# Block products with seven multiplications in layer 1 of a routed MLP, with layer 2 computed for two experts at a time

## The chip, the cores and the metric

One core of a Trainium2 chip. The metric is the device time of one execution in microseconds, the median over runs. A profile is one such execution with every instruction recorded; its span is about 2 us shorter than the time. The granted clock is the share of TensorE's full clock that the profile records; "half clock" below means that it was 0.5.

Names used below: PE is TensorE (matmuls), PEld its weight loads, DVE is VectorE, ACT is ScalarE, POOL is GpSimd, SP is SyncE, which issues DMAs.

## The reference

Sliding-window attention (8 batches of 576 tokens, 8 heads of 64) gives x, 4608 tokens by 512. Then a dense mixture of 8 experts, weighted by a matrix P that eight rounds of row and column normalisation (Sinkhorn) produce:

```python
P = np.exp(logits - logits.max())
for _ in range(8):
    P /= P.sum(1, keepdims=True) + 1e-09
    P /= P.sum(0, keepdims=True) + 1e-09
    P *= N / E
for e in range(8):
    h = np.maximum(x @ w1[e], 0.0)      # layer 1: 512 -> 1024
    out += P[:, e:e + 1] * (h @ w2[e])  # layer 2: 1024 -> 512
```

## The kernel before

Expert 0 is computed during and just after the attention, without P. Then experts 1 to 7 run over 9 groups of 512 tokens: 63 steps. In a step, layer 1 of the *next* step is woven between the products of layer 2 of this one. P is positive, so x is multiplied by it before layer 1. Layer 2 already uses the Winograd form of Strassen's method: hidden activations and w2 are cut into 2 x 2 blocks, and seven block products instead of eight give the result, with sums S (S1 to S4) of activations and T of weights made on DVE. `rebase` takes one quarter of a group's running result off another quarter, so that the products can be added to it; `settle` adds it back at the end.

```python
def make_xs(i):                      # x * P, P in fp32
    for d2 in range(2):
        nc.vector.tensor_tensor(out=xss[i][:, 2*d2:2*d2+2, :], in0=xT[:, 2*d2:2*d2+2, ...],
                                in1=Pb.unsqueeze(1).to_broadcast([P, 2, GT]), op=ALU.mult)

def l1s(i, ft):                      # layer 1, plain: 8 x 4 matmuls of 512 columns a step
    for dt in range(NDT):
        nc.tensor.matmul(out=psh, lhsT=w1ts[e][:, dt, P*ft:P*ft+P], rhs=xss[i][:, dt, :], ...)
    nc.scalar.activation(out=hTs[i][:, ft, :], in_=psh, func=AF.Relu)

def product(i, m):                   # layer 2: one of seven products, 8 matmuls of 256 columns
    ...

def gather(i, bank, rh, ch, op):     # add a product's bank to the running result
    if (rh, ch) != (1, 1) and e < E - 1:
        nc.scalar.copy(out=st, in_=banks[bank])                # ACT: PSUM -> SBUF
        nc.gpsimd.dma_start(out=t, in_=st, accum_op=ALU.add)   # DMA adds
        return
    nc.vector.tensor_tensor(out=t, in0=t, in1=banks[bank], op=op)
# [cut] the loop: product 1, piece of layer 1, product 7, piece, 5, piece, 6, piece, 2, ...
```

The whole kernel:

The softmax here doesn't subtract the row's maximum and nothing guards it: scores larger than these inputs give would overflow.

## Time and profile before

| | |
|---|---|
| time | 1088.22 us (6 runs, 1084.86 to 1091.17) |
| span of the profile | 1083.1 us |
| attention, up to the last gate matmul | 207.8 us |
| first layer-1 matmul of expert 1 | 250.8 us |
| one step | 13.02 us |
| last layer-1 matmul; last matmul | 1066.2; 1073.8 us |

The page's first lines give busy time, share of the span and instructions per engine:

```profile
span 1083.1 us, 18767 instructions
## 1 busy us (share of the span) xinstructions
PE 1047.4 (97%) x7675; PEld 670.9 (62%) x7675; DVE 694.1 (64%) x1072; ACT 542.7 (50%) x959; POOL 270.2 (25%) x264
```

The chain of waits, followed back from the last instruction, as the page sums it up by engine:

```profile
PE 93%; DVE 2%; DMA 1%; ACT 1%; issue 1%; DVEq 0%; POOL 0%; ACTq 0%; SPq 0%; POOLq 0%
```

And two pieces of the same chain in order of time (start, duration, engine, what and line), the runs of eight layer-1 matmuls where one step meets the next:

```profile
569.27 1.73 PE psh L577 x8
582.29 1.73 PE psh L577 x8
```

So TensorE bounds the kernel, and a step is 582.29 - 569.27 = 13.02 us.

Groups of instructions (line, engine, operation, output and inputs, shapes, count; busy us and mean ns of one; idle time just before them and what ended it):

```profile
L577 PE MATMUL psh<-xs,w1t 128*128 128x512 f16 x2016 | 506.3, 379 | 0.5 <-DVE xs L564 0.5
...
L649 ACT COPY st<-M 128x512 f32<-128x512 f32 x162 | 94.0, 580 | 0.0
...
L564 DVE TENSOR_TENSOR xs<-xT,Pb 128x1024 f16<-128x1024 f16 x126 | 148.2, 1218 | 1.0 <-DMA Pb<-PTd 1.0
...
L601 DVE TENSOR_TENSOR S<-hT 128x1024 f16<-128x1024 f16 x126 | 86.7, 688 | 198.9 <-ACT hT L584 198.9
...
L652 DVE TENSOR_TENSOR acc_lo<-acc_lo,M 128x512 f32<-128x512 f32 x186 | 127.1, 683 | 61.6 <-PE M L635 61.6
```

The stretches view of the steady loop (stretch, length, then busy us and instructions of PE, PEld, DVE, ACT, POOL; granted clock, DMA share, GB/s):

```profile
400.00:500.00 100.00, 100.00 (x677) 65.95 (x675) 59.45 (x82) 46.52 (x85) 29.02 (x25) 1.00 0.53 87
```

PE never stops there; DVE and ACT have 40% and 53% of their time free. That free time is what the change spends.

### The profile page before, as it was taken

The page shows a single profiled execution, that of the slowest core. Times are in us where ns is not written, and L with a number is a line of the kernel's source. Part 1 is how long each engine was busy: PE and PEld are TensorE (multiplying, and loading weights), DVE is VectorE, ACT ScalarE, POOL GpSimd, SP SyncE. Part 2 cuts the span into 40 slices and gives each one's busy share as a digit, 9 for nine tenths or more (in the row PEclk, how much of TensorE's full clock was granted, in tenths as well). Part 3 has the DMA queues.
Part 4 walks back from the last instruction along what each step waited for, and adds up shares of the span by engine and source line. Part 5 has one row for each costly group of instructions (what it writes and reads, how often), then busy time and mean ns, then how long its engine had stood idle before and what let it go on. Part 6 is the DMA issues. An engine that isn't in the chain of part 4 may idle for free.

```text
span 1083.1 us, 18767 instructions
## 1 busy us (share of the span) xinstructions
PE 1047.4 (97%) x7675; PEld 670.9 (62%) x7675; DVE 694.1 (64%) x1072; ACT 542.7 (50%) x959; POOL 270.2 (25%) x264
## 2 busy tenths in 40 slices
PE   4899999899999999999999999999999999999996
PEld 2655555445666666666666666666666666666664
DVE  5877776656666755565556555565556555667885
ACT  3666666456666544444444444444444444443331
POOL 6332230010332322223222323232222323220000
PEclk9999999999999999999999999999999999999998
DMA  9978761424455594449444765559444944443323
GB/s 172 158 77 77 72 67 8 81 32 111 80 85 84 90 159 79 79 78 155 80 82 84 124 121 85 83 85 156 79 78 79 156 79 85 83 61 105 104 93 97
DMA packets 123334, 101.36 MB, mean 94 GB/s; under 512 B 46288, under 2 KB 107120, under 8 KB 123248
## 3 DMA queue, kind: packets, MB, share of 16 engines
q0 software_dynamic: 107968, 73.44, 50.8%
q1 hardware_dynamic: 14848, 26.34, 7.8%
q8 instruction: 60, 0.98, 0.4%
q10 hardware_dynamic: 432, 0.39, 0.1%
q14 instruction: 26, 0.21, 0.1%
HBM read 79.02 MB, written 9.58 MB: 82 GB/s over the span
## 4 chain that ended last, share of the span: by engine, by line
PE 93%; DVE 2%; DMA 1%; ACT 1%; issue 1%; DVEq 0%; POOL 0%; ACTq 0%; SPq 0%; POOLq 0%
PE psh L577 40%; PE M L635 35%; PE psh L110 6%; PE psy L124 5%; PE psS L219 3%; PE psN L267 2%; ACT pt L227 1%; PE psT_q L187 1%; PE psT_k L187 1%; PE psXT L307 1%; DMA qf<-in_q_dram 1%; DVE xsb L276 1%; DMA PTd<-PT_sb 0%; DVE acc_hi L652 0%; DVE QZ L206 0%
## 5 line engine op out<-in xcount | busy, mean ns | idle before, releaser
L584 ACT ACTIVATE hT<-psh 128x512 f16<-128x512 f32 x504 | 301.9, 599 | 424.9 <-PE psh L577 423.3
L577 PE MATMUL psh<-xs,w1t 128*128 128x512 f16 x2016 | 506.3, 379 | 0.5 <-DVE xs L564 0.5
L577 PEld LDWEIGHTS <-w1t 128*128 128x128 f16 x2016 | 197.2, 98 | 145.9 <-issue 0.8
L635 PEld LDWEIGHTS <-S 128*128 128x128 f16 x2016 | 197.2, 98 | 75.8
L601 DVE TENSOR_TENSOR S<-hT 128x1024 f16<-128x1024 f16 x126 | 86.7, 688 | 198.9 <-ACT hT L584 198.9
L650 POOL DMA_DIRECT2D acc_lo<-st x108 | 128.8, 1211 | 339.7 <-ACT st L649 339.2
L635 PEld LDWEIGHTS <-hT 128*128 128x128 f16 x1512 | 147.9, 98 | 59.3 <-issue 3.1
L652 DVE TENSOR_TENSOR acc_lo<-acc_lo,M 128x512 f32<-128x512 f32 x186 | 127.1, 683 | 61.6 <-PE M L635 61.6
L564 DVE TENSOR_TENSOR xs<-xT,Pb 128x1024 f16<-128x1024 f16 x126 | 148.2, 1218 | 1.0 <-DMA Pb<-PTd 1.0
L635 PE MATMUL M<-w2t,S 128*128 128x256 f16 x1008 | 130.6, 273 | 0.0
L635 PE MATMUL M<-w2t,hT 128*128 128x256 f16 x1008 | 130.6, 273 | 0.0
L635 PE MATMUL M<-T,S 128*128 128x256 f16 x1008 | 130.5, 273 | 0.0
L650 POOL DMA_DIRECT2D acc_hi<-st x54 | 64.4, 1204 | 170.1 <-ACT st L649 167.7
L649 ACT COPY st<-M 128x512 f32<-128x512 f32 x162 | 94.0, 580 | 0.0
L652 DVE TENSOR_TENSOR acc_hi<-acc_hi,M 128x512 f32<-128x512 f32 x93 | 63.5, 683 | 29.4 <-PE M L635 29.1
L227 ACT ACTIVATE pt<-psS 128x1024 f16<-128x1024 f32 (+2 forms) x80 | 68.2, 852 | 16.5 <-PE psS L219 15.4
L110 PE MATMUL psh<-xT,w1t 128*128 128x512 f16 x288 | 70.0, 384 | 1.6 <-ACT P_sb L299 1.1
L124 PE MATMUL psy<-w2t,hT 128*128 128x512 f16 x288 | 66.6, 379 | 0.8 <-ACT P_sb L299 0.8
L635 PE MATMUL M<-T,hT 128*128 128x256 f16 x504 | 65.3, 273 | 1.2 <-DVE acc_hi L652 1.2
L117 ACT ACTIVATE hT<-psh 128x512 f16<-128x512 f32 x72 | 43.1, 598 | 24.7 <-PE psh L110 24.0
L219 PE MATMUL psS<-QZ,KT 128*128 128x512 f16 (+2 forms) x160 | 45.3, 365 | 8.3 <-ACT pt L227 7.3
L235 DVE TENSOR_TENSOR pt<-pt,maskT 128x1024 f16<-128x1024 f16 (+2 forms) x80 | 45.9, 574 | 5.7 <-ACT pt L227 5.4
(61 smaller groups left out, 636.2 us busy)
## 6 DMA issues: line engine op xcount, KB each, us to landing
acc_lo<-st POOLq DMA_DIRECT2D x108, 256.0 KB, 4.0
Pb<-PTd SPq DMA_DIRECT2D x63, 256.0 KB
acc_hi<-st POOLq DMA_DIRECT2D x54, 256.0 KB, 3.9
w2t<-in_moe_w_dram POOLq DMA_DIRECT2D x8, 1024.0 KB, 15.9
w1t<-in_moe_w_dram POOLq DMA_DIRECT2D x7, 1024.0 KB, 9.8
out_dram<-acc_lo SPq DMA_DIRECT2D x48, 128.0 KB
kf<-in_k_dram POOLq DMA_DIRECT2D x16, 288.0 KB, 5.5
qf<-in_q_dram POOLq DMA_DIRECT2D x16, 288.0 KB, 6.7
```

The source lines that it names most:

```text
L110: nc.tensor.matmul(out=psh, lhsT=w1t[:, dt, P * ft : P * ft + P], rhs=xT[:, dt, GT * g : GT * g + GT], start=(dt == 0), stop=(dt == NDT - 1),)
L124: nc.tensor.matmul(out=psy, lhsT=hT[:, ft, P * ms : P * ms + P], rhs=w2ts[e][:, ft, :], start=(ft == 0), stop=(ft == NFT - 1),)
L219: nc.tensor.matmul(out=ps[0:nk, jj, :, 0:nq], lhsT=KT[:, 2 * half + jj, k0 : k0 + nk], rhs=QZ[:, 2 * half + jj, :, k0 : k0 + nq],)
L227: nc.scalar.activation(out=pt[0:nk, :, 0:nq], in_=ps[0:nk].rearrange("p a b q -> p (a b) q")[:, :, 0:nq], func=AF.Exp, scale=scale,)
L564: nc.vector.tensor_tensor(out=xss[i][:, 2 * d2 : 2 * d2 + 2, :], in0=xT[:, 2 * d2 : 2 * d2 + 2, GT * g : GT * g + GT], in1=Pb.unsqueeze(1) ...
L577: nc.tensor.matmul(out=psh, lhsT=w1ts[e][:, dt, P * ft : P * ft + P], rhs=xss[i][:, dt, :], start=(dt == 0), stop=(dt == NDT - 1),)
L584: nc.scalar.activation(out=hTs[i][:, ft, :], in_=psh, func=AF.Relu)
L601: nc.vector.tensor_tensor(out=t, in0=a, in1=b, op=op)
L635: nc.tensor.matmul(out=ps[:, ms, :], lhsT=a[:, kt, P * ms : P * ms + P], rhs=b[:, kt, :], start=(first and ms == 0 and kt == 0), stop=(kt ...
L649: nc.scalar.copy(out=st, in_=banks[bank])
L650: nc.gpsimd.dma_start(out=t, in_=st, accum_op=ALU.add)
L652: nc.vector.tensor_tensor(out=t, in0=t, in1=banks[bank], op=op)
```

## The change: its intent and the diff

Intent: use the seven-product form for layer 1 too. Three kinds of work follow.

1. Layer 1 becomes 7 products per half of its output rows (`dp`), 56 matmuls of 256 columns instead of 32 of 512 per step. The ReLU is not linear, so all four result blocks must be complete in PSUM before it. Three PSUM banks (la, lb, lc) and one SBUF tile (m5) hold them, with two ACT copies and two DVE adds in each half. DVE makes the sums of weights (`ws`) per expert and differences of x (`xd`) per step.
2. To make room, experts 2 and 3, 4 and 5, 6 and 7 share one layer 2 with an inner dimension of 2048. Its PE work per expert is unchanged, but results are gathered half as often.
3. To make room in SBUF, x is no longer kept there: it is written to DRAM during the attention and read back, 512 KB a step. P is sent as fp16.

```diff
-    xT = per.tile([P, NDT, Ntok], FP16, name="xT")
+    xTd = nc.dram_tensor("xTd", [NG * P, NDT * GT], FP16, kind="Internal").ap()
+        def load_x(key, g: int):
+            xls[key] = msb.tile([P, NDT, GT], FP16, name=f"xl_{key}", tag="xl", bufs=2)
+            nc.sync.dma_start(out=xls[key], in_=x_dram(g))
-            Pbs[i] = msb.tile([P, GT], FP32, name=f"Pb_{e}_{g}", tag="Pb", bufs=3)
+            Pbs[j] = msb.tile([P, GT], FP16, name=f"Pb_{e}_{g}", tag="Pb", bufs=2)
+        def chunk(j, n):                       # one of 8 chunks of layer 1 of step j
+            dp, c = divmod(n, 4)
+            if c == 0:
+                l1_product(j, dp, 1)           # PE -> la
+                nc.scalar.copy(out=lbanks["lb"], in_=lbanks["la"])
+                l1_product(j, dp, 5)           # PE -> ld
+                nc.scalar.copy(out=m5, in_=lbanks["ld"])
+            elif c == 1:
+                l1_product(j, dp, 6)           # PE adds to lb: after the ACT copy
+                l1_product(j, dp, 2)           # PE adds to la
+                tt(out=lbanks["lc"], in0=lbanks["lb"], in1=m5s[j], op=ALU.add)
+                l1_relu(j, dp, lbanks["la"], 0, 0)
+            elif c == 2:
+                l1_product(j, dp, 7)           # PE adds to lb: after DVE has read it
+                l1_product(j, dp, 3)           # PE adds to lc
+                tt(out=m5s[j], in0=lbanks["lb"], in1=m5s[j], op=ALU.add)
+                l1_relu(j, dp, lbanks["lc"], 0, 1)
+                l1_relu(j, dp, m5s[j], 1, 1)
+            else:
+                l1_product(j, dp, 4)           # PE adds to lb: after DVE has read it
+                l1_relu(j, dp, lbanks["lb"], 1, 0)
+        tasks = [(1, g) for g in range(NG)]    # expert 1 alone, then pairs
+        for p in range(2, E, 2):
+            tasks += [(p + kh, g) for g in range(NG) for kh in range(2)]
```

(A slot is a place between two chunks; slot 3 follows the first multiply of x, just before the second half of layer 1 needs DVE.) Between the attention and the experts, layer 1 of two groups of expert 0 moves ahead of the Sinkhorn rounds.

## The prediction

> **What bounds it now.** TensorE. In the chain of waits PE is 93%; the expert loop alone is 75% (layer 1 40%, layer 2 35%). In the stretches view PE is always busy from 300 to 1000 us, clock 1.00. It repeats every 13.02 us (chain: 569.27, 582.29): 32 layer-1 matmuls of 512 columns (eight take 1.73 us: 0.216 each, 6.92) and 56 layer-2 matmuls of 256 columns, the remaining 6.10, 0.109 each. Cost follows columns.
>
> **Removed.** Layer 1 of experts 1 to 7 becomes seven block products instead of eight: 56 matmuls of 256 columns, 6.10 us for 6.92. Ideal step 12.2 us; 63 steps give 52 us. On the chain. Layer 2 keeps its PE work; pairing two experts halves its result handling (279 DVE adds of 683 ns, 162 ACT copies of 580 ns, as many accumulating DMAs), off the chain.
>
> **Added (busy time per step).**
> - DVE: two PSUM adds per half, 4 x 683 ns = 2.7 us; four block differences of x, 4 x about 0.42 = 1.7 (estimated from 274, 549 and 684 ns of 256, 768 and 1024). Multiplying x by the routing weight becomes all fp16: 2 x 684 instead of 2 x 1218 ns. "VectorE: DVE Perf Modes" of the Trainium skill (mode 2x_1P) says two results per cycle need 16-bit data; the trace agrees: 684 ns for 1024 all-fp16 elements, 1218 with an fp32 operand. Sum: about 10 us of 12.2 in a paired step.
> - ACT: 4 copies, 2.3 us; sum about 8 us.
> - Expert 1 (unpaired, also rescaling) is the tightest: both near 11.7 us by busy time; it should just fit, as back-to-back starts are 0.1 us closer than durations.
> - x is read back, 512 KB a step, while accumulating DMAs fall from 162 to about 100.
>
> **Will the new waits show?** Each chunk of layer 1 crosses PE to ACT or DVE and back before the next. From the timeline: about 0.26 us from the end of a matmul's slot to the reader's start, 0.58 to 0.68 us of work, 0.13 back: about 1.0 to 1.07 us. Between lie 0.435 us of product and 0.87 of layer 2. Slack 0.2 to 0.3 us. Placing a pair of steps by hand leaves PE without waits, if x lands within 6 us of issue.
>
> **Losses (estimates).** Transition 4 us (six rebase subtractions, 4 us, now precede the copy of the routing weights on DVE; the first chunks run back to back); two thin steps between expert 1 and the first pair, 3; expert 1, 2; weight transforms displacing adds, 3; late x or weight loads, 2 to 3.
>
> **Predicted.** 1088 - 52 + 14 = 1050 us, 8 in 10 in 1036 to 1072. Faster by over 2%: 0.84; within 2%: 0.13; slower: 0.03.
>
> **What would show it.**
> - Loop step 12.2 to 12.5 us, 24.4 to 25 per pair; PE busy above 97% there at clock 1.00.
> - Layer 1: 2016 matmuls of 512 columns become 3528 of 256, 273 ns each.
> - DVE busy about 75 to 85% in the loop, ACT about 65%; PE waits for DVE or ACT inside layer 1 sum to under 15 us.
> - First loop step starts 3 to 7 us later than now.
>
> **What would make it wrong.** PSUM-to-PSUM adds or copies slower than 0.68 and 0.58 us; DVE late for the adds: 0.15 us in each of six exchanges a step eats the gain. x landing late. PE losing its clock to gaps.

## The result, and the profile after

| | before | after |
|---|---|---|
| time, median | 1088.96 us (16 runs) | 1050.04 us (8 runs, 1047.44 to 1051.36) |
| ratio of fast runs | | 0.9644, 95% interval 0.9630 to 0.9658 |
| span of the profile | 1083.1 | 1048.9 |
| last gate matmul | 207.8 | 211.2 |
| first layer-1 matmul of expert 1 | 250.8 | 252.7 |
| steady step | 13.02 | 12.23 |
| last layer-1 matmul; last matmul | 1066.2; 1073.8 | 1028.2; 1040.8 |

A ratio is the mean time of one kernel's fast runs over that of the other's of the same rounds, so it is not quite the ratio of the medians.

The page's first lines and the chain of the kernel after:

```profile
span 1048.9 us, 22435 instructions
## 1 busy us (share of the span) xinstructions
PE 1004.4 (96%) x9187; PEld 818.9 (78%) x9187; DVE 799.8 (76%) x1355; ACT 642.7 (61%) x1151; POOL 199.8 (19%) x208
...
PE 59%; DVE 3%; issue 0%; ACT 0%; POOL 0%; POOLq 0%; DVEq 0%
```

The chain's 59% isn't a fall of PE's part: this chain could be followed back only to 380.8 us, so its shares add up to about 62% of the span. Inside it nearly everything is still PE.

The stretches view, expert 1 first, then two of the pairs:

```profile
300.00:380.00 80.00, 76.96 (x685) 66.28 (x684) 73.50 (x129) 63.09 (x116) 23.58 (x21) 1.00 0.83 157
400.00:500.00 100.00, 99.47 (x912) 89.01 (x910) 73.88 (x116) 60.57 (x110) 14.07 (x12) 1.00 0.40 87
600.00:700.00 100.00, 99.62 (x914) 89.13 (x912) 77.64 (x119) 60.66 (x110) 15.07 (x13) 1.00 0.52 109
```

In the pairs PE is still busy 99.5% of the time and DVE 74 to 78%; in expert 1 DVE is at 92% and ACT at 79% (73.50 and 63.09 of 80), and PE loses 3 us in 80. The groups:

```profile
L650 PE MATMUL lb<-xl,w1t 128*128 128x256 f16 x504 | 75.6, 272 | 3.5 <-DVE lc L685 3.4
...
L650 PE MATMUL lb<-xd,w1t 128*128 128x256 f16 x504 | 75.6, 272 | 3.2 <-DVE m L690 3.1
...
L592 DVE TENSOR_TENSOR xl<-xl,Pb 128x1024 f16<-128x1024 f16 x126 | 86.1, 683 | 5.6 <-DMA Pb<-PTd 5.6
...
L685 DVE TENSOR_TENSOR lc<-lb,m 128x512 f32<-128x512 f32 x126 | 88.0, 698 | 93.2 <-PE lb L650 91.5
...
L676 ACT COPY lb<-la 128x512 f32<-128x512 f32 x126 | 71.9, 570 | 32.8 <-PE la L650 30.0
...
L680 ACT COPY m<-ld 128x512 f32<-128x512 f32 x126 | 74.7, 593 | 0.0
...
L763 DVE TENSOR_TENSOR acc_lo<-acc_lo,M 128x512 f32<-128x512 f32 x96 | 65.2, 679 | 1.0 <-PE lb L650 0.5
```

The multiply by P takes 683 ns instead of 1218, as its operands are now all fp16. The new PSUM-to-PSUM operations take 698 ns (DVE) and 570 ns (ACT), within 3% of the PSUM operations that the trace of before had.

One exchange in a steady step, from the timeline (start, duration, engine, what; brackets: idle before and what ended it):

```profile
699.98 0.60 PE L650 MATMUL la<-xl,w1t 128*128 128x256 f16 x4
...
711.77 0.60 PE L650 MATMUL lb<-xd,ws 128*128 128x256 f16 x4
...
712.21 0.60 PE L650 MATMUL la<-xl,w1t 128*128 128x256 f16 x4
...
712.48 0.70 DVE L685 TENSOR_TENSOR lc<-lb,m 128x512 f32<-128x512 f32 x1 [0.79 <-PE lb L650]
...
712.64 1.04 PE L752 MATMUL M<-w2t,S 128*128 128x256 f16 x8
...
713.52 0.60 PE L650 MATMUL lb<-xl,w1t 128*128 128x256 f16 x4
```

The first line is the matmul group of the step before that corresponds to the one at 712.21, one step of 12.23 us earlier. PE hands lb over at 712.21, where its next matmul group starts. DVE starts 0.27 us later and ends at 713.18. PE comes back to lb at 713.52, 0.34 us after that, so it doesn't wait (where PE does wait for this add elsewhere in the trace, it starts 0.05 us after DVE's end, so the slack is about 0.29 us). DVE had stood idle for 0.79 us before. This is how the hand-overs of layer 1 hide behind layer 2: the way out takes 0.97 us (712.21 to 713.18), and 1.31 us of other matmuls stand between.

**Where the time went.** I took the start-to-start times of all matmuls of both traces and counted what exceeds 0.216 us (512 columns) or 0.109 us (256 columns) as a wait; waits after the experts begin add up to 14 us. The ledger of the two profiled runs:

| term | us |
|---|---|
| 63 steps x (13.02 - 12.226) us | -50.0 |
| first chunks of layer 1, back to back, and waiting for x*P: waits 3.2 instead of 0.6 | +2.6 |
| expert 1, five steps, four of them 12.72 to 13.33 us: waits before product 7 of layer 2 (the sum S3 is late) and at lb | +3.1 |
| start of the first pair, 367 to 402 us | +6.3 |
| starts of the other two pairs, steps of 12.87 and 12.77 us, two each | +2.4 |
| the last expert and the end of layer 2: waits 2.2 before, 0.3 after | -1.9 |
| last matmul to the end: 9.2 before, 8.1 after | -1.1 |
| attention and the next 16 us at half clock for longer in this run: 3.4 + 1.0 | +4.4 |
| sum | -34.2 |

The spans differ by 34.2 us and the medians by 38.9: the profiled execution of before is the fastest of its 16 runs (1084.86 us), with an early rise of the clock, and that of after (1050.67) is an ordinary one with a late rise. The experiments' last part comes back to this.

### The profile page after: what moved, and what is told of

It reads as the page before. It is cut to its first block, busy times and chain, and to the rows that moved or that the text cites. A ratio compares the mean times of both kernels' runs of the same rounds, so it can differ in the third digit from the quotient of the medians.

```text
span 1048.9 us, 22435 instructions
## 1 busy us (share of the span) xinstructions
PE 1004.4 (96%) x9187; PEld 818.9 (78%) x9187; DVE 799.8 (76%) x1355; ACT 642.7 (61%) x1151; POOL 199.8 (19%) x208
## 4 chain that ended last, share of the span: by engine, by line
PE 59%; DVE 3%; issue 0%; ACT 0%; POOL 0%; POOLq 0%; DVEq 0%
PE M L752 30%; PE lb L650 13%; PE la L650 8%; PE ld L650 4%; PE lc L650 4%; DVE lc L685 1%; DVE m L690 0%; DVE T L789 0%; DVE hT L728 0%; DVE w2t L789 0%; DVE xd L609 0%; DVE S L730 0%; DVE acc_hi L763 0%; DVE ws L626 0%; DVE S L732 0%
## 5 line engine op out<-in xcount | busy, mean ns | idle before, releaser
L752 PEld LDWEIGHTS <-hT 128*128 128x128 f16 x2504 | 245.0, 98 | 28.4
L650 PEld LDWEIGHTS <-ws 128*128 128x128 f16 x1512 | 147.8, 98 | 19.0 <-issue 1.6
L685 DVE TENSOR_TENSOR lc<-lb,m 128x512 f32<-128x512 f32 x126 | 88.0, 698 | 93.2 <-PE lb L650 91.5
L650 PE MATMUL la<-xl,w1t 128*128 128x256 f16 x1008 | 151.2, 273 | 0.8 <-PE psy L128 0.8
L690 DVE TENSOR_TENSOR m<-lb,m 128x512 f32<-128x512 f32 x126 | 87.0, 690 | 46.5 <-PE lb L650 45.2
L752 PEld LDWEIGHTS <-S 128*128 128x128 f16 x1024 | 99.7, 98 | 15.1 <-DVE S L726 3.1
L592 DVE TENSOR_TENSOR xl<-xl,Pb 128x1024 f16<-128x1024 f16 x126 | 86.1, 683 | 5.6 <-DMA Pb<-PTd 5.6
L661 ACT ACTIVATE hT<-lb 128x512 f16<-128x512 f32 x126 | 75.6, 600 | 14.8 <-PE lb L650 14.6
L661 ACT ACTIVATE hT<-m 128x512 f16<-128x512 f32 x126 | 78.5, 623 | 2.6 <-DVE m L690 2.6
L650 PE MATMUL lb<-xl,w1t 128*128 128x256 f16 x504 | 75.6, 272 | 3.5 <-DVE lc L685 3.4
```

The source lines that it names most:

```text
L592: tt(out=x, in0=x, in1=Pbs[j].unsqueeze(1).to_broadcast([P, 2, GT]), op=ALU.mult)
L650: nc.tensor.matmul(out=ps[:, f, :], lhsT=a[:, kt, f0 : f0 + P], rhs=b[:, kt, :], start=(m in (1, 5) and f == 0 and kt == 0), stop=(kt == 1 ...
L661: nc.scalar.activation(out=hTs[j][:, f0 : f0 + 2, T2 * th : T2 * th + T2], in_=src, func=AF.Relu)
L685: tt(out=lbanks["lc"], in0=lbanks["lb"], in1=m5s[j], op=ALU.add)
L690: tt(out=m5s[j], in0=lbanks["lb"], in1=m5s[j], op=ALU.add)
L752: nc.tensor.matmul(out=ps[:, ms, :], lhsT=a[:, kt, P * ms : P * ms + P], rhs=b[:, kt, :], start=(new and ms == 0 and kt == 0), stop=(kt == ...
```

## The experiments

"Step" below is the distance between the first layer-1 matmuls of successive steps in the trace.

### Plain layer 1, all else kept

```diff
-            if c == 0:
-                l1_product(j, dp, 1) ...
+            for dt in range(NDT):
+                nc.tensor.matmul(out=psh, lhsT=w1ts[e][:, dt, P*n:P*n+P], rhs=xls[j][:, dt, :], ...)
+            nc.scalar.activation(out=hTs[j][:, n, :], in_=psh, func=AF.Relu)
-                make_xd(...), make_ws(...)          # no differences, no weight sums
```

> The changed kernel with layer 1 of experts 1 to 7 computed plainly again (32 matmuls of 512 columns a step), all else kept: pairs of experts, x read back, fp16 routing weights, new hand-over between attention and experts. Theory (the gain is the eighth of layer-1 columns, all on TensorE): the step goes back from 12.23 to 13.02 us, plus 50 us over 63 steps, minus the 10 to 12 us of waits inside block layer 1 that vanish: 1084 to 1094 us, ratio to the kernel before 0.997 to 1.005. Rival (pairing, with half the result handling and fewer accumulating DMAs, or the fp16 multiply gave a good part): clearly under 1075 us.

Measured: 1085.96 us, ratio 0.9968 (0.9946 to 0.9989), a hair under the expected 0.997. Two successive runs of eight layer-1 matmuls in its chain:

```profile
572.76 1.73 PE psh L675 x8
...
585.78 1.73 PE psh L675 x8
```

Steady steps are 13.02 us, and the waits fall from 14 us to 0.5. The theory holds: block layer 1 by itself carries the gain, 1085.96 to 1050.04; everything else in the change together is worth about 2.4 us by the medians, 1 to 6 us by the interval of the ratio.

### The kernel before, with only P in fp16

```diff
-    PTd = nc.dram_tensor("PTd", [E * NBLK, P], FP32, kind="Internal").ap()
+    PTd = nc.dram_tensor("PTd", [E * NBLK, P], FP16, kind="Internal").ap()
```
(and the two tiles PT_sb and Pb in the same way)

> The kernel before with only the routing weights sent and read as fp16, so that the multiply of x is all fp16 (0.68 us instead of 1.22, 67 us of VectorE work less). Theory (TensorE never waits for it): same within 0.3%, at most 0.5 us from a multiply that ends sooner at the start of the experts. Rival (VectorE relief carried gain): 3 us or more faster.

Measured: 1085.83 us against 1088.38, ratio 0.9973 (0.9952 to 0.9994). It is within the 0.3% of the theory, but the expected 0.5 us was too low: 2.5 us, and the interval leaves out 1 by a hair. The trace shows 1.5 us of it. In before, the last expert's steps are 13.14 us, not 13.02 (a wait of 0.12 us in each of seven), and the first multiply is waited for by 0.64 us; both waits are gone. The two profiled spans don't show it (1083.3 us here, 1083.1 in before): this trace has half clock for 6.8 us after the attention and not 3.4, and its first layer-1 matmul of expert 1 starts 1.7 us later. "PE never waits for DVE" was true of the loop, but not of the last expert, whose results DVE gathers too.

### Block layer 1 without pairing

The schedule of expert 1 is used for all experts; the weight transforms go one by one into slot 3 of the eight steps before an expert.

```diff
-        for p in range(2, E, 2):
-            tasks += [(p + kh, g) for g in range(NG) for kh in range(2)]
+        tasks = [(e, g) for e in range(1, E) for g in range(NG)]
-                self.pair = self.e > 1
+                self.pair = False
+            for n in range(4):
+                at(h - 8 + n, 3, make_ws, e, (1, 2, 3, 4)[n])
+                at(h - 4 + n, 3, make_t, e, (0, 3, 1, 2)[n])
```

> The changed kernel with block layer 1 but without pairing: every expert's layer 2 alone as before, the schedule of the first expert used for all, weight transforms one per step in the gap before the second half. Theory A (pairing is off the chain, and its start costs 6.3 us in the first and 1.2 us in each later pair): steps stay at 12.23 us, the pair starts go, 1040 to 1047 us, and accumulating DMAs rise to about 165. Theory B (pairing is what makes room on VectorE and ScalarE for block layer 1): VectorE at about 90% busy is late for its exchanges, steps of 12.5 to 12.8 us as in the second half of expert 1, 1060 to 1085 us.

Measured: 1092.66 us, ratio 1.0037 (1.0016 to 1.0057), which taken alone would speak for theory B, or worse. The trace says otherwise. The stretches view:

```profile
600.00:700.00 100.00, 100.00 (x918) 89.64 (x917) 88.61 (x154) 65.42 (x121) 30.64 (x27) 1.00 0.75 142
```

PE is busy all of the time with DVE at 89%. All 47 steps from the 11th to the 57th are 12.23 us, across every change of expert. Only the last expert fails, with steps of 20.3 to 22.9 us. Its timeline:

```profile
970.05 1.01 PE L647 MATMUL lb<-xl,w1t 128*128 128x256 f16 x4 [7.98 <-DVE lc L682]
...
973.32 1.29 DVE L788 TENSOR_TENSOR acc_lo<-acc_lo 128x512 f32<-128x512 f32 x2
...
974.07 8.88 SPq L76 DMA_DIRECT2D out_dram<-acc_lo  x8
...
978.85 0.60 PE L647 MATMUL lb<-xl,w1t 128*128 128x256 f16 x4
...
983.05 0.39 SPq L483 DMA_DIRECT2D xl<-xTd  x1
...
983.49 0.43 SPq L581 DMA_DIRECT2D Pb<-PTd  x1
...
989.01 0.69 DVE L589 TENSOR_TENSOR xl<-xl,Pb 128x1024 f16<-128x1024 f16 x1 [7.45 <-DMA Pb<-PTd]
```

My schedule put eight stores of results ahead of the next loads on the same SP queue. They wait for DVE's last additions (973.32), take 8.88 us to issue, and only then do x and P get issued; DVE idles for 7.45 us, and TensorE with it. In the steady steps x is issued 2.0 us before a step begins, in the last expert 7.6 to 9.7 us after. The stalls cost more than their own length: the five waits at lb are 6.0 to 8.2 us by matmul starts, 33.7 us together, and around each of them the granted clock falls to 0.5 for 6.8 to 10.2 us (the four matmuls at 970.05 take 1.01 us, those at 978.85, at full clock, 0.60). The slower matmuls make another 10.3 us. The mean granted clock of this run is 0.975.

### Unpaired, loads ahead of stores

```diff
                     if k == 6:
                         Unit(h + 1).make_s(3)
+                        load_next(h)
                         if unit.e == E - 1 and 0 < g < NG - 1:
                             put_out(g - 1)
                     extra()
-                load_next(h)
```

> The unpaired kernel with one edit: in the last expert the loads of x and of the routing weights are issued before the stores of the result on the same SyncE queue, not after. Theory (pairing was not what was missing; loads queued behind stores that wait for VectorE held TensorE for 8 to 10 us in each of five steps): those steps fall from 20 to 23 us to at most 15, 1048 to 1065 us. Rival (too much DMA traffic or VectorE work in the last expert without pairs): the steps stay near 20 us.

One look: 1051.0 us, state unknown. Timed again:

> The unpaired kernel with loads first again, timed, since the first look was one run of unknown state: 1048 to 1052 us, ratio to the kernel before 0.963 to 0.967, the same as the changed kernel within 0.3%.

Measured: 1051.78 us, ratio 0.9657 (0.9644 to 0.9671). The last expert's steps are 12.52 us. So the queue order was the whole failure, 41 us with the half clock that its stalls brought, and block layer 1 doesn't need pairing for its exchanges. What is left in the last expert, 0.3 us a step, is a wait at lb for DVE, which has two settling additions (1.28 us) in its queue that the other steps don't have; DVE doesn't wait for x or P there. Waits are about 10 us instead of 14, as there are no pair starts, but 12.2 to 12.7 us pass from the last matmul to the end instead of 6.9 to 8.1: with pairs a group of 512 tokens is finished every 24.5 us, here every 12.2, and its stores follow. That this is why the end is longer is not shown.

### Unpaired, results settled later and stored from two queues

```diff
-                        if unit.e == E - 1 and 0 < g < NG - 1:
-                            put_out(g - 1)
+                    if k == 3 and unit.e == E - 1:
+                        out_10(g - 1)      # half of the group before, stores on SP and POOL
+                        out_01(g - 2)      # the other half of the one before that
```

> The unpaired kernel with the results of the last expert settled one and two groups later, in the gap of VectorE ahead of the second half of layer 1, and stored half from SyncE and half from GpSimd, so that the loads of x are not held up. Theory (block layer 1 needs no pairing): all steps near 12.23 us to the end, no pair starts (8.7 us of waits in the changed kernel), 1038 to 1046 us, 3 to 10 us under the changed kernel. Rival (VectorE at 89% can't carry the settling too): last expert at 13 to 14 us a step, 1046 to 1056 us.

Measured: 1058.49 us, ratio 0.9731 (0.9706 to 0.9757); steps of the last expert 12.9 to 16.8 us. Neither number fits. Stores in the middle of a step again come before the loads at its end: in the trace the loads are issued at 975.95 and 976.40, and the multiply that needs them starts at 985.76. Their order in the queue is the smaller part: x is issued 1.0 to 2.6 us before the steps with stores, where the steady steps have 2.0. The transfers are slow: in the step looked at, the last piece of P moves 9.2 us after the issue of x, with 190 pieces of 2 KB, the stores', on the same queue in between; in a step of the loads-first kernel it is 7.1 us, in the paired one 3.5.

### Unpaired, loads first, tail and base subtractions moved

```diff
-            store(4 * g + 2)
+            store(4 * g + 2, engs=(nc.sync, nc.gpsimd))     # groups 5 to 7, all stores
-                        if h + 1 >= g0:
-                            rebase(h + 1, 1)
+        for n, g in enumerate(range(g0, NG)):
+            at(n // 2, 3, rebase, g, 1)
-                at(h - 8 + n, 3, make_ws, e, (1, 2, 3, 4)[n])
+                at(h - 7 + n, 3, make_ws, e, (1, 2, 3, 4)[n])
```

(The last edit, weight sums one step later, is not in the text of the expectation.)

> The unpaired kernel with loads first, and two more edits: the last groups' stores leave half from SyncE and half from GpSimd, which has no accumulating DMA left there, and the second base subtraction of groups 6 to 8 moves into the gap of VectorE in the first two steps. In the run without them 12.2 us passed from the last matmul to the end (6.9 in the changed kernel) and three steps of expert 1 took 12.72 us. Theory: the tail falls to 7 to 9 us and the three steps to 12.25: 4 to 6 us faster than that run, 1043 to 1047 us, so the unpaired form is 3 to 7 us under the changed kernel. Rival (the stores are limited by what moves, not by the queue): no change in the tail, 1049 to 1051 us.

Measured: 1049.12 us, ratio 0.9635 (0.9622 to 0.9648). Two of the three slow steps became 12.23 us, one stayed at 12.71, and an earlier one grew from 12.23 to 12.37. The tail hardly moved, 11.6 us for 12.2-12.7: there the rival's number was right, and the second issuing engine bought little; what does limit the tail is not shown. Paired and unpaired forms end within 1 us of each other, each with its own loss.

### Extra work on VectorE

```diff
                 make_xd(j, 1)
+                for _ in range(5):     # or 2; the same difference again
+                    tt(out=xds[j][:, 0], in0=x_quad(j, 0, 1), in1=x_quad(j, 0, 0), op=ALU.subtract)
```

> The changed kernel with five extra copies of the first block difference of x (128x512 fp16, about 0.34 us from start to start, same result), 1.7 us of VectorE a step, placed just ahead of the exchange that opens the second half of layer 1. Reading of the trace: VectorE is idle for about 0.9 us there and TensorE has about 0.2 us of slack, so 0.6 us a step comes through, about 35 us in all: 1075 to 1095 us, and the gaps stand before the lb matmuls. Rival (VectorE has 25% of the step free, so 1.7 of 12.2 us fits): under 1055 us.

Measured: 1115.87 us, ratio 1.0246 (1.0224 to 1.0268), above the range. The paired steps went from 12.23 to 13.03 and 13.09 us, but an extra operation that rewrites the same tile took 0.46 us from start to start, not 0.34, so 2.3 us were added; expert 1 and the pair starts, with no gap left, lengthened more, most of their steps to 13.3 to 14.8 us. A paired step (the extra operations, the add that they delay, the wait of TensorE), and the stretches view:

```profile
706.06 2.26 DVE L810 TENSOR_TENSOR xd<-xl 128x512 f16<-128x512 f16 x5
...
709.44 0.69 DVE L685 TENSOR_TENSOR lc<-lb,m 128x512 f32<-128x512 f32 x1
...
710.19 0.60 PE L650 MATMUL lb<-xl,w1t 128*128 128x256 f16 x4 [0.71 <-DVE lc L685]
...
600.00:700.00 100.00, 91.03 (x822) 80.12 (x820) 89.37 (x153) 54.68 (x100) 16.38 (x15) 1.00 0.61 117
```

The rival, that free DVE time anywhere in the step is enough, is out: DVE was about 77% busy in the pairs, so some 2.8 us of a step looked free, more than the 2.3 us added. Nor is it the busy share that decides: DVE is 89% busy both here and in the unpaired kernel, and TensorE is busy for 91% of the time here and for 100% there.

> The changed kernel with two extra block differences instead of five. In the run with five they took 0.46 us each, 2.3 us, and the paired steps went from 12.23 to 13.06. Theory (a gap of about 0.98 us on VectorE, then about 0.2 us of slack, both used up before TensorE waits): two, 0.92 us, cost nothing in the paired steps (12.23 to 12.27 us), and only the second half of expert 1 and the starts of the pairs lengthen: 1050 to 1062 us. Rival (each added microsecond costs in proportion, 0.36 us per us): steps of 12.56, about 1072 us.

Measured: 1051.57 us, ratio 0.9665 (0.9647 to 0.9683); the paired steps away from the starts stay at 12.23 us but for one of 12.26; the steps just before the two later pair starts take 12.26 and 12.25. DVE's timeline in a paired step shows the gap filled up:

```profile
707.29 0.88 DVE L810 TENSOR_TENSOR xd<-xl 128x512 f16<-128x512 f16 x2
...
708.37 0.70 DVE L685 TENSOR_TENSOR lc<-lb,m 128x512 f32<-128x512 f32 x1 [0.20 <-PE lb L650]
```

0.92 us of DVE work cost nothing in a paired step, and 2.3 us cost 0.83: about 1.5 us (2.3 - 0.83) is what the gap and PE's slack absorb at this place.

### The change again, and small work moved into the gap

> The changed kernel itself once more, for a second trace and a ratio on this chip. Expected: 1047 to 1051 us, steps again 12.23 us with waits of about 14 us at the same places (start of the experts, second half of expert 1, starts of the pairs); the stretches at half clock in the attention part fall elsewhere, since they differ between the two traces at hand.

Measured: 1049.8 us, ratio 0.9646 (0.9629 to 0.9664). Steps and waits repeat to 0.02 us, at the same places; the stretches at half clock are others.

The ledger said that the waits in expert 1 and at the first pair are DVE work standing ahead of an exchange. To test that, and to win it:

```diff
-                        if h + 1 >= g0:
-                            rebase(h + 1, 1)
+        for n, g in enumerate(range(g0, NG)):
+            at(n // 2, 3, rebase, g, 1)
-                    at(2 + n, 5, make_ws, e, m)
+                    at(2 + n, 3, make_ws, e, m)
-                at(h, 1, make_t, p, 0)
-                at(h, 4, make_t, p, 3)
-                at(h, 6, make_t, p, 1)
+                at(h - 3, 3, make_t, p, 0)     # with a buffer of its own for expert 1's T0
+                at(h - 2, 3, make_t, p, 3)
+                at(h, 1, make_t, p, 1)
```

> The changed (paired) kernel with small VectorE work moved into the gap ahead of the second half of layer 1 (0.98 us, by the run with two extra differences): the second base subtraction of groups 6 to 8 into steps 0 and 1, the weight transforms of expert 2 one slot earlier in steps 2 to 5, and two of the four layer-2 transforms of the first pair three and two steps earlier (one of them with a buffer of its own). Theory (the waits left in expert 1 and at the first pair are VectorE work that sits ahead of an exchange, so moving it removes the wait): the three steps of 12.72 and the one of 13.3 us go to 12.23 to 12.4, the sum of the four thin steps falls from 49.6 us by 2 to 4: 1043 to 1047 us, ratio to the kernel before 0.957 to 0.961. Rival (these waits come from the thin steps having too little layer 2 between exchanges, whatever VectorE does): only the 2.5 us in expert 1 are won.

Measured: 1044.57 us, ratio 0.9601 (0.9588 to 0.9614), the best of all and under both kernels. The steps that took 12.72, 12.72, 12.72 and 13.33 us take 12.23, 12.23, 12.23 and 12.47; the four at the first pair fall from 49.6 to 47.5 us in sum, of which 0.5 is the last of expert 1's waits. One step of expert 1 grew from 12.23 to 12.36. One wait of 1.09 us for the DVE add stays at the first pair:

```profile
376.14 0.60 PE L650 MATMUL lb<-xl,w1t 128*128 128x256 f16 x4 [1.09 <-DVE lc L685]
```

In these steps layer 2 is only half as long (expert 1's last unit is spread over two steps), so the thin steps may keep a part of their waits whatever DVE does, as the rival has it. No run separates the two: two of the transforms and the weight sums of expert 3 still stand there.

**The clock in the attention part.** Over thirteen traces the last gate matmul falls between 207.8 and 212.3 us. The trace records when the granted clock rises for good in the attention: at 39.6 to 39.7 us in three of them, which end at 207.8 to 208.5 (before, before with fp16 P, and one unpaired kernel whose attention is that of the change), and at 46.8 to 49.8 us in the others, which end at 209.5 to 212.3. The 512-column matmuls of the scores take 0.58 to 0.635 us in the slow stretches and 379 ns in the fast ones. Since one kernel with the change's attention has the early rise, the change doesn't rule it out; why it is rarer there is open.

## Why the prediction was right or wrong

The time, 1050 us, was met by the median of 1050.04, and the mechanism is shown by the run with plain layer 1. That the sum is right to 0.1 us is luck: the single terms below miss by up to 3.3 us, and their errors, with two terms that weren't foreseen, cancel.

- **"Removed ... 52 us"**: 50.0. The step is 12.23 us, not 12.2. I took 0.2163 us per matmul from a rounded 1.73; the two measured steps (32a + 56b = 13.02, 112b = 12.226) give 0.2158.
- **"Will the new waits show?"**: right in the pairs, the step that mattered most. Durations (570, 593, 690, 698 ns) and hand-over (0.27 us) are as assumed, and the steady step has no wait. The slack by hand was 0.2 to 0.3 us; the timeline shows 0.29 (0.34 less a way back of 0.05, which the prediction took as 0.13). The run with five extra operations, beside the unpaired one, shows that the position of a free stretch counts, not its share.
- **DVE "75 to 85%", ACT "about 65%", waits "under 15 us"**: 72 to 84% in stretches of 100 us among the pairs, 60 to 62%, 14 us.
- **"First loop step starts 3 to 7 us later"**: 6.2 (the second group of layer 1 begins at 265.40, before at 259.23), of which 3.4 were lost in the attention.
- **"Expert 1 ... 2"**: 3.1; **"weight transforms ... 3"**: 2.4 at the later pairs.
- **"two thin steps ... 3"**: 6.3. I had counted the shorter layer 2, but not that the weight transforms of the first pair fall in the same steps. This was the largest miss. The last experiment wins back about 1.6 us of it by moving two of them into earlier steps and a third within its step.
- **"Transition 4 us (six rebase subtractions ...)"**: 2.6 us, and by another mechanism. The subtractions ended at 242.1 us, but the transposes before the copy had been issued only at 240.8, behind layer 1 of expert 0. Waiting for P (4.0 us of DVE idle) and the back-to-back chunks made the waits.
- **"late x or weight loads, 2 to 3"**: none to speak of. The multiply of x waited for a DMA five times in all, 5.6 us of DVE's time, of which 4.0 at the start of the experts. The unpaired kernels show that this holds only while stores don't stand in front of the loads.
- **Not foreseen**: 3.0 us gained at the end (the last expert's waits and the tail), and the clock in the attention.
- **Pairing "off the chain"**: right. Without it all steps from the 11th to the last expert's are 12.23 us. What it does buy is at the end: last steps of 12.23 us for 12.52 with loads first, and a shorter tail. The output leaves over 220 us rather than 110, and x and P land 3.5 us after issue, not 7.1; but the 12.52 is a wait for DVE, as shown above, and not for these loads.

What the prediction named as a danger, "PE losing its clock to gaps", did not happen in the change, whose gaps in the expert loop are 1.3 us at most; it did in the unpaired kernel, around gaps of 6.0 to 8.2 us, and in the one that settled later, around two of its gaps of 2.8 to 2.9 us.

What stays open: what limits the tail of the unpaired kernels (a second issuing engine hardly helped), and what sets the moment of the clock's rise.

## What to carry to other kernels

When one engine is saturated and the others are not, trading its work for hand-overs pays if every round trip fits into the work that stands between, so compare the hand-over (here about 1.0 us) with that work (1.3 us), place by place, and move every other operation of the helping engine into its own gaps; a helper at 89% busy hid everything in one kernel, and at 89% again, with 2.3 us more at a single place, it cost TensorE 9% of its time in another. Read a surprising total by steps before believing it: the unpaired kernel was slower than the one before, yet 47 of its steps in a row ran without a wait, and one reordered line in a DMA queue was worth 41 us, about a quarter of it from the clock that fell after each stall. Extra loads hide only while nothing that waits stands ahead of them in their issuing queue.

## What the Trainium skill lacked or had wrong

- "DMA: Bandwidth & Descriptors", section "Issuing engines are not separate DMA queues", says that issuing from several engines only saves the sequencer's issue time, which is usually small. The order of one issuing queue was not small here: eight stores took 8.88 us to issue ahead of two loads, and putting the loads first took the kernel from 1092.66 to 1051.78 us. No page puts a cost on loads that stand behind waiting or slow stores in one issuing queue. The run with stores issued from a second engine (tail 11.6 us for 12.2 to 12.7) agrees with the section.
- "Perfetto Trace Analysis", section "Identifying the Most-Contended Engine", recommends LDWEIGHTS busy time, beside the share of peak FLOPs, as a measure of headroom on TensorE. In the two steady stretches it is 66% before and 89% after, while the matmuls follow each other without gaps in both (PE busy 100% and 99.5%): it followed the width of the matmuls, 512 or 256 columns per weight load, not the headroom.
- "ScalarE: Activation LUTs", section "Step-by-step: what each stage is for", notes that ScalarE writes faster to PSUM than to SBUF; the note itself has no figure. The trace agrees, by a little: the copy from PSUM to PSUM took 570 ns, and that to SBUF 593, same shape.
- "VectorE: DVE Perf Modes", section "The DRAIN you can't avoid", says that the next operation does not start until the pipe is empty, and that one that is not held starts earlier. It has no figure for an operation that rewrites the tile of the one before it. Here 128x512 fp16 differences into the same tile started 0.46 us apart, 0.03 us after the end of a record of 0.42, where unrelated ones started 0.08 us before it.
- "TensorE: Matmul & The Clock Gate", section "What's actually happening", says that the ramp of the clock costs under 1% of a typical kernel and varies between runs. The runs agree (end of the attention 207.8 to 212.3 us, 0.4% of the time), but in a study of steps of 2 to 5 us that is noise of the size of what is sought, and should be read off the trace each time.
